# A new written-out order of the same work, and another choice of which engine scales which row

## The chip, the cores and the metric

The kernel runs on one core of a Trainium2 chip. The core has a matrix engine (PE, with its weight loads shown apart as PEld), a vector engine (DVE), an activation engine (ACT), GpSimd (POOL), a queue engine (SP), and sixteen DMA engines that move data between HBM and the on-chip memory. The metric is the device time of one execution in microseconds. Three executions of the kernel before took 898.75, 900.19 and 900.25 us, so its median is 900.19 us.

## The reference

The input `x` has 2048 tokens of width 576. Two results are made of it and mixed token by token with a gate:

```python
g = _sigmoid((x * gate_w).sum(-1, keepdims=True))
a = irfft2(rfft2(x) * (w_r + 1j * w_i))          # over tokens and width
q = einsum("nd,dhc->nhc", x, w_q)                # 32 heads, 2 x 128
s1, s2 = q1 @ k1.T, q2 @ k2.T                    # 64 scores each
e = argmax(s1) * 64 + argmax(s2)                 # one of 4096 experts
act = gelu(einsum("nd,nhd->nh", x, u[e]))
b = einsum("nh,nh,nhd->nd", softmax_of_one, act, v[e])
return g * a + (1 - g) * b
```

Part `a` is a two-dimensional Fourier filter. Part `b` picks, for each token and each of 32 heads, one row of `u` and one row of `v`, takes the dot product of the token with the `u` row, and sums the `v` rows weighted by the result. The softmax is over a single candidate.

## The kernel before

The 2048 tokens are 16 tiles of 128. The heads are cut into 8 chunks of 4. Each `u` row is stored next to its `v` row, so that one gather brings both: 128 rows of 1152 numbers, 4608 bytes each, into a slot called `uv`. There are 512 such gathers, one for each tile and head.

**Scores.** For each chunk `c`, `build_m` (L345 to L356) multiplies the query weights with the keys, and `scores` (L406) multiplies the token tiles with the result, two tiles at a time (`tp`). ACT and DVE find the index of the largest score (L415 to L453).

**Tiles 0 to 9** (`group`, L516 to L577). Four gathers are issued by POOL (L516), four dot products are taken on DVE (L523, "dots"), ACT applies gelu (L525), and the four `v` rows are weighted and summed. `ROWS[t][c]` says how. The value 16 means that PE sums them, with diagonal weights that ACT makes (L563). Otherwise bit k of the value means that row k is scaled on ACT (L548) and then added on DVE (L549); a bit that is not set means that DVE scales and adds in one instruction (L553). Tiles 0 and 1 (`T_T`) take another way in both kernels: ACT scales (L499), PE turns the rows and sums them in PSUM (`turned`), and DVE adds the result (L506).

**Tiles 10 to 15** (`quad`, L604 to L641). Here a gather holds four heads of 32 tokens. The indices are turned for that by sixteen small copies on ACT (`shuffle`, L462). The token tile is repeated (`repeat`, PE L594 and ACT L596). Then come the gathers (L604), the dots (L609), gelu (L610), the weights `a` (L611), a small diagonal `dg` (L613), and sixteen matmuls (L625) that add four rows to the sum of the tile. These last matmuls free the four `uv` slots.

**The filter.** `fold` (DVE L743 to L745, PE L752, ACT L754 and L755) prepares each of the 16 token tiles. When all are folded, `f2` (L764) begins the transform, followed by `f4`, `f5` and `f6` for each frequency group, and by `invert` (L904 and L914, with DVE L907 and L908) for each tile. `gates` (DVE L332) takes the dot product for the gate. `mix` (L930) joins both parts, `send` (L934) stores a tile, and `finish` (L639 to L641) does this in two halves for tile 15.

**The order.** All of this is first written down as 4337 jobs, numbered as they are created. The list `ORDER` holds the 4337 numbers. `follow` walks this list. Every engine carries out its own jobs strictly in the order of the list (each is tied to the one before it on its engine by a dependency without a semaphore); between engines only data and slots make one wait for another. The walk also hands out the slots: a job that needs a slot takes the one that has been free for longest in the list:

```python
for n, x in enumerate(seq):
    j = self.jobs[x]
    for b in j.bufs:
        if b.tag is None:
            b.tag = next(g for g in b.tags if self.rings.get(g))
            b.slot = self.rings[b.tag].popleft()
    for b in j.bufs:
        b.left -= 1
        if not b.left:
            self.rings[b.tag].append(b.slot)
```

So a change of the list changes which job of an engine comes first, and which earlier job a gather waits for before its slot is free. In the last third of the execution there are 18 `uv` slots: 12 of their own, two in areas that are free by then (one of them is shown in the profile as `area`), and four that held token tiles until their gates were taken (shown as `pair`).

The jobs that the prediction speaks of have these numbers in both lists: 3246 is the first matmul job of the filter's transform (`f2`, q = 0); 3495 to 3510 are the gate dots of tiles 0 to 15; 4283 is the PE job of tile 15, chunk 3; 4272 to 4275 are the four gathers of that chunk; 4276 to 4279 are their dots, 4281 is `a` and 4282 is `dg`; 4287 and 4291 are the gather and the dot of row 3 of chunk 4; 3627, 3662 and 3582 are the first PE jobs of `invert` for tiles 10, 15 and 5.

Of the kernel before, what the change touches and what calls it, by code (L numbers as in the profile page):

```python
# [969 lines left out]
ROWS = {0: (0, 16, 16, 15, 6, 2, 12, 0), 1: (0, 15, 0, 12, 5, 16, 5, 16), 2: (12, 8, 2, 6, 0, 8, 0, 1), 3: (2, 10, 0, 5, 0, 7, 4, 16), 4: (4, 0, 0, 6, 16, 7, 16, 0), 5: (2, 0, 1, 0, 0, 9, 12, 16), 6: (4, 15, 4, 8, 16, 0, 16, 14), 7: (8, 0, 16, 16, 6, 12, 9, 2), 8: (6, 16, 7, 0, 12, 16, 16, 11), 9: (4, 0, 0, 16, 0, 8, 16, 5)}  # L970
# [19 lines left out]
def is_d(t, c):  # L990
    return t < NE and ROWS[t][c] > 15


ORDER = [
# [214 lines left out]
```

## Time and profile before

| | us |
|---|---|
| median of three executions | 900.19 |
| the profiled execution, as timed | 900.38 |
| its span, from the first to the last instruction | 898.6 |
| PE busy | 856.3 |
| DVE busy | 811.5 |
| ACT busy | 596.3 |
| POOL busy | 570.3 |

The profiled execution lies 0.19 us above the median. Between its span and its time lie 1.8 us. Busy times are unions of the instructions' records; consecutive matmuls overlap in the records, so a PE that is shown as fully busy is fed without a gap, but a single matmul's duration is longer than the distance to the next one. A stretch in the table of windows shows, for each engine, its busy time and number of instructions, then the granted share of the PE clock, the mean busy share of the sixteen DMA engines and the rate in GB/s.

### The profile page before, as it was taken

How to read it: one execution, taken by the hardware profiler on the slowest of the kernel's cores; microseconds unless marked ns; L12 is line 12 of the kernel's file. 1: busy time of each engine (PE TensorE's matmuls, PEld its weight loads, DVE VectorE, ACT ScalarE, POOL GpSimd, SP SyncE). 2: the span in 40 equal slices, each digit the busy share in tenths (PEclk: the TensorE clock that was granted, in tenths of full speed). 3: DMA queues.
4: the chain of work that ended last, by engine and by line, in shares of the span. 5: the costliest groups of instructions: out<-in, count | busy, mean ns of one | idle time of the engine just before them, and what ended most of it. 6: DMA issues, size and time to landing. Idle time of an engine off the chain costs nothing. (4 is left out here: it accounts for less than half of the span.)

```text
span 898.6 us, 16947 instructions
## 1 busy us (share of the span) xinstructions
PE 856.3 (95%) x5502; PEld 661.0 (74%) x5502; DVE 811.5 (90%) x2022; ACT 596.3 (66%) x2067; POOL 570.3 (63%) x516
## 2 busy tenths in 40 slices
PE   6999999999999999999999999769889999899987
PEld 5888888888888778888888888657556676566554
DVE  3779999999999899999999999899999889877877
ACT  4999997877878688788879789773232434232322
POOL 0356556666677676676657776666767677777771
PEclk9999999999999999999999999859999999999999
DMA  9999999999999999999999999999999999999998
GB/s 299 349 332 367 379 345 367 349 372 361 380 357 368 377 386 384 376 388 357 394 359 368 415 350 397 418 370 365 402 415 420 419 402 419 420 420 419 418 419 340
DMA packets 89611, 342.44 MB, mean 381 GB/s; under 512 B 9969, under 2 KB 10865, under 8 KB 89522
## 3 DMA queue, kind: packets, MB, share of 16 engines
q0 software_dynamic: 73728, 302.02, 86.5%
q1 hardware_dynamic: 15794, 39.33, 11.9%
q8 instruction: 44, 0.72, 0.3%
q14 instruction: 45, 0.37, 0.1%
HBM read 336.59 MB, written 4.72 MB: 380 GB/s over the span
## 5 line engine op out<-in xcount | busy, mean ns | idle before, releaser
L516 POOL DMA_INDIRECT uv<-uv,ei x317 | 356.6, 1125 | 226.5 <-issue 46.6
L260 PE MATMUL bank<-mh,xt 128*128 128x512 f32 x768 | 269.8, 402 | 0.0
L422 ACT ACTIVATE area<-bank,area 128x64 bf16<-128x64 f32 x1008 | 220.3, 360 | 15.1 <-DVE area L415 10.9
L604 POOL DMA_INDIRECT uv<-uv,eiq x144 | 156.6, 1087 | 70.1 <-issue 23.3
L523 DVE SCALAR_TENSOR_TENSOR uv<-uv,pair 128x576 f32<-128x576 f32 x256 | 187.3, 750 | 12.5 <-DMA uv<-uv,ei 11.9
L260 PE MATMUL bank<-ml,xt 128*128 128x512 f32 x448 | 175.0, 391 | 0.0
L260 PEld LDWEIGHTS bank<-mh,xt 128*128 128x128 f32 x768 | 144.2, 188 | 30.3
L260 PE MATMUL bank<-mhx,xt 128*128 128x512 f32 x384 | 136.6, 399 | 0.1
L260 PE MATMUL bank<-uv,dg 128*32 128x288 f32 (+1 forms) x784 | 115.0, 412 | 4.3 <-DVE dg L613 4.2
L609 DVE SCALAR_TENSOR_TENSOR uv<-uv,xr 128x576 f32<-128x576 f32 x144 | 105.7, 751 | 12.4 <-DMA uv<-uv,eiq 12.1
L553 DVE SCALAR_TENSOR_TENSOR xn<-uv,a,xn 128x576 f32<-128x576 f32 x133 | 107.7, 811 | 0.2
L260 PE MATMUL bank<-fi,bt 128*128 128x289 f32 x384 | 101.7, 416 | 1.0 <-DVE area L908 1.0
L260 PEld LDWEIGHTS bank<-fi,bt 128*128 128x128 f32 x384 | 82.5, 243 | 20.6 <-issue 6.5
L260 PEld LDWEIGHTS bank<-ml,xt 128*128 128x128 f32 x448 | 84.3, 188 | 15.7
L260 PEld LDWEIGHTS bank<-uv,dg 128*32 128x32 f32 (+1 forms) x784 | 60.6, 131 | 35.7 <-DVE dg L613 10.1
L260 PEld LDWEIGHTS bank<-mhx,xt 128*128 128x128 f32 x384 | 72.1, 188 | 15.6 <-DVE area L371 0.5
L415 DVE TENSOR_REDUCE area<-bank 128x16 f32<-128x1024 f32 x63 | 76.6, 1217 | 4.3 <-PE bank L260 4.0
L260 PE MATMUL bank<-mlx,xt 128*128 128x512 f32 x192 | 75.0, 390 | 0.0
L430 ACT ACTIVATE area<-area 128x256 bf16<-128x256 bf16 x189 | 73.0, 437 | 1.1
L610 ACT ACTIVATE b<-z 128x4 f32<-128x4 f32 x48 | 9.9, 205 | 84.4 <-DVE uv L609 57.9
L260 PEld LDWEIGHTS bank<-kT,uv 128*64 128x64 f32 x1280 | 41.6, 141 | 18.2 <-issue 13.4
L260 PE MATMUL bank<-kT,uv 128*64 128x64 f32 x1280 | 46.5, 228 | 6.7 <-DMA uv<-wqT 6.7
(199 smaller groups left out, 1348.1 us busy)
## 6 DMA issues: line engine op xcount, KB each, us to landing
uv<-wqT SPq DMA_DIRECT2D x32, 512.0 KB, 6.5
uv<-uv,ei POOLq DMA_INDIRECT x317, 6.9
w<-wri SPq DMA_DIRECT2D x16, 289.0 KB, 6.7
pair<-xn SPq DMA_DIRECT2D x8, 288.0 KB, 6.2
uv<-uv,eiq POOLq DMA_INDIRECT x144, 8.6
out<-xn SPq DMA_DIRECT2D x8, 288.0 KB, 5.8
uv<-wq SPq DMA_DIRECT2D x8, 256.0 KB, 6.5
uv<-xT SPq DMA_DIRECT2D x8, 256.0 KB, 7.1
```

The lines of the kernel that those rows point to most:

```text
L260: after('PE', nc.tensor.matmul(*args, **kw))
L415: dv(dve(1024, True), lambda: nc.vector.tensor_reduce(mv.ap[:, 2 * tp:2 * tp + 2, :], ps.ap.rearrange('p a (g e) -> p a g e', e=E), AX.X, ...
L422: on('ACT', actv(sg.ap[:, j, g, :], ps.ap[:, j, g * E:g * E + E], AF.Sign, bias=mv.ap[:, 2 * tp + j, g:g + 1], scale=-1.0))
L430: ac(act(256), lambda b=b: actv(s2()[:, :, b * Q:b * Q + Q], s2()[:, :, b * Q:b * Q + Q], AF.Copy, bias=b / 4), [sg], [])
L516: on('POOL', nc.gpsimd.indirect_dma_start(out=g.ap.rearrange('p a d -> p (a d)'), out_offset=None, in_=uv, in_offset=bass.IndirectOffsetOn ...
L523: dv(0.68, lambda k=k, g=rows[k]: stt(g.ap[:, 0, :], g.ap[:, 0, :], 1.0, x.ap, op0=ALU.mult, op1=ALU.mult, accum_out=z.ap[:, k:k + 1]), [( ...
L553: dv(0.73, lambda v=v, s=s: stt(y.ap, v(), s(), y.ap, op0=ALU.mult, op1=ALU.add), [y], [(rows[k], 1), a])
L604: on('POOL', nc.gpsimd.indirect_dma_start(out=g.ap.rearrange('p a d -> p (a d)'), out_offset=None, in_=uv, in_offset=bass.IndirectOffsetOn ...
L609: dv(0.68, lambda j=j: stt(rows[j].ap[:, 0, :], rows[j].ap[:, 0, :], 1.0, xr[t][j].ap, op0=ALU.mult, op1=ALU.mult, accum_out=z.ap[:, j:j + ...
L610: ac(0.1, lambda: actv(b.ap, z.ap, AF.Gelu_apprx_tanh), [b], [(z, j) for j in range(HPC)], table='gelu')
```

## The change

Only two constants differ. In `ROWS`, 30 of the flags of tiles 2 to 9 are changed: 15 rows that ACT scaled are now scaled and added by DVE alone, and 15 go the other way. The number of flagged rows is 61 in both kernels, no entry of 16 appears or goes, and the entries of tiles 0 and 1 stay as they are. `ORDER` is another permutation of the same 4337 jobs; all 173 of its lines differ.

```diff
-ROWS = {0: (0, 16, 16, 15, 6, 2, 12, 0), 1: (0, 15, 0, 12, 5, 16, 5, 16), 2: (12, 8, 2, 6, 0, 8, 0, 1), 3: (2, 10, 0, 5, 0, 7, 4, 16), 4: (4, 0, 0, 6, 16, 7, 16, 0), 5: (2, 0, 1, 0, 0, 9, 12, 16), 6: (4, 15, 4, 8, 16, 0, 16, 14), 7: (8, 0, 16, 16, 6, 12, 9, 2), 8: (6, 16, 7, 0, 12, 16, 16, 11), 9: (4, 0, 0, 16, 0, 8, 16, 5)}
+ROWS = {0: (0, 16, 16, 15, 6, 2, 12, 0), 1: (0, 15, 0, 12, 5, 16, 5, 16), 2: (12, 2, 2, 6, 4, 2, 0, 1), 3: (2, 10, 0, 0, 0, 7, 6, 16), 4: (2, 0, 0, 6, 16, 7, 16, 8), 5: (2, 0, 3, 8, 6, 9, 12, 16), 6: (4, 5, 0, 9, 16, 0, 16, 12), 7: (8, 0, 16, 16, 6, 9, 9, 2), 8: (0, 16, 6, 8, 12, 16, 16, 10), 9: (4, 0, 8, 16, 0, 4, 16, 5)}
...
 ORDER = [
-    21, 22, 0, 1, 23, 2, 3, 77, 4, 78, 9, 16, 6, 10, 89, 90, 80, 7, 5, 79, 133, 20, 91, 11, 13, 81, 83, 84, 128, 92, 97, 82, 86, 87, 8, 98, 85, 17,
...
+    3608, 3588, 4295, 3596, 3587, 4303, 4314, 3581, 4304, 4305, 3666, 4306, 4316, 3563, 3543, 3890, 4317, 4307, 3597, 4318, 4326, 3598, 3633, 3599,
+    4328, 4329, 4330, 4222, 4223, 3778, 4319, 3589, 3668, 3779, 3590, 3667, 4331, 4334, 4332, 4335, 4333, 4336,
 ]
```

What stands where in the two lists can be counted from them. Counted per engine, the median job of PE and of POOL moves by 2 places among the jobs of its engine, the median job of DVE and of ACT by 3. Jobs of each engine listed ahead of some jobs (before / after):

| ahead of | PE | DVE | ACT | POOL |
|---|---|---|---|---|
| the last job of the scores (tile 14) | 820 / 820 | 923 / 925 | 871 / 873 | 298 / 300 |
| 3246, the first job of `f2` | 853 / 854 | 1038 / 1040 | 971 / 974 | 328 / 331 |
| the first sum of tile 12 | 909 / 908 | 1217 / 1209 | 1063 / 1059 | 397 / 397 |
| the first sum of tile 14 | 961 / 962 | 1363 / 1364 | 1139 / 1142 | 462 / 461 |
| 4283, the sum of tile 15, chunk 3 | 1001 / 1000 | 1464 / 1461 | 1193 / 1192 | 506 / 510 |

343 rows, old and new, of the table ORDER are left out of this document.

## Prediction

> **What bounds the kernel now.** I read the page's first line and the list of waits, then the table of windows, and then the timelines at the two places where the table shows that something breaks.
>
> ```profile
> span 898.6 us, 16947 instructions
> PE bank L260 <- DMA uv<-wqT: 6.7, 1, 6.7
> ...
> 270.00:360.00 90.00, 89.78 (x567) 73.30 (x566) 85.03 (x203) 71.90 (x267) 59.75 (x53) 1.00 0.99 379
> ...
> 450.00:540.00 90.00, 90.00 (x519) 73.71 (x515) 87.67 (x216) 73.69 (x286) 60.76 (x56) 1.00 0.99 373
> ```
>
> PE waits 6.7 us for its first weights and is then fed almost without a gap until 540 us; the poorer of these two windows lacks 0.22 us in 90, and it is the poorest. An order can't do better there with the same matmuls, only worse. What is left to win lies behind 540 us, in 358 us.
>
> ```profile
> 540.00:560.00 20.00, 19.23 (x120) 16.69 (x118) 19.31 (x51) 18.16 (x65) 12.51 (x12) 1.00 1.01 395
> 560.00:580.00 20.00, 15.34 (x92) 12.68 (x92) 16.46 (x49) 17.41 (x72) 13.02 (x13) 0.99 1.03 416
> 580.00:600.00 20.00, 12.34 (x52) 10.24 (x52) 20.00 (x52) 12.74 (x40) 11.07 (x11) 0.59 0.98 370
> 600.00:611.00 11.00, 9.89 (x47) 6.58 (x45) 10.30 (x29) 7.75 (x23) 6.44 (x6) 0.53 1.00 379
> 611.00:630.00 19.00, 18.15 (x110) 14.60 (x106) 17.99 (x54) 7.51 (x30) 14.44 (x14) 1.00 0.97 372
> 630.00:675.00 45.00, 39.15 (x232) 26.17 (x233) 44.04 (x114) 14.00 (x36) 31.49 (x30) 1.00 1.02 409
> 675.00:720.00 45.00, 44.72 (x271) 30.91 (x270) 40.38 (x103) 15.84 (x37) 32.46 (x30) 1.00 1.03 420
> 720.00:855.00 135.00, 130.64 (x811) 85.00 (x810) 110.62 (x308) 45.42 (x117) 101.89 (x93) 1.00 1.02 416
> 855.00:877.00 22.00, 17.69 (x103) 11.08 (x102) 16.13 (x46) 5.00 (x14) 15.40 (x16) 1.00 1.03 418
> 877.00:898.60 21.60, 16.13 (x119) 8.71 (x117) 17.00 (x46) 6.06 (x17) 3.19 (x3) 0.96 0.85 337
> ```
>
> Three stages are to be seen. From 560 to 611 us the scores are over, PE idles for 13.4 us (51 less 15.34, 12.34 and 9.89), its clock is granted at about half, and DVE is full from 580 on: DVE is late with the folds, and `f2` can't begin before the last of them. From 630 to 877 us the DMA engines are busy all the time and move 409 to 420 GB/s, where the two windows of the scores above have 379 and 373; gathers are the bound there. Behind 877 us the last rows are summed.
>
> **The change part by part.** `ROWS` moves 30 flags and leaves their number at 61. A row scaled by DVE alone costs 811 ns, one scaled on ACT costs DVE 750 ns:
>
> ```profile
> L553 DVE SCALAR_TENSOR_TENSOR xn<-uv,a,xn 128x576 f32<-128x576 f32 x133 | 107.7, 811 | 0.2
> L549 DVE TENSOR_TENSOR xn<-uv,xn 128x576 f32<-128x576 f32 x60 | 44.9, 750 | 1.3 <-ACT uv L548 1.2
> ```
>
> Fifteen rows go each way, 15 x 0.06 = 0.9 us of DVE out and in, so this sums to nothing; what hides it besides is PE, the bound of the stage where nearly all these rows lie. If that cover is gone it costs or brings up to 0.9 us.
>
> *Up to 560 us* I put 0. The first three loads on SP (the fifth weight block, the keys, the first weight block) are the same in both lists, so PE starts at 6.7 us again; and at the last score job both lists have 820 PE jobs behind them, with 923 and 925 on DVE. Below there is only the 0.22 us quoted. Above: DVE has 2.3 to 5 us of slack in each 90 us window; an order that let PE wait for 1% of that stage would cost 5 us. I take 0, being nearest to the rows.
>
> *The folds, 560 to 611 us.* DVE sets the end, so I count its jobs ahead of job 3246: 1038 before, 1040 after. By line, two gate dots (L332) and one dot (L609) more, and one tiny L449 less. Consecutive dots start 0.68 us apart (first two rows); the other rows are DVE's waits for gathers between 540 and 611 us (total, times, longest) and the start of `f2`:
>
> ```profile
> 608.28 0.75 DVE L332 SCALAR_TENSOR_TENSOR pair<-pair,t 128x576 f32<-128x576 f32 x1
> ...
> 608.96 0.75 DVE L332 SCALAR_TENSOR_TENSOR pair<-pair,t 128x576 f32<-128x576 f32 x1
> DVE uv L523 <- DMA uv<-uv,ei: 2.7, 3, 1.1
> 610.94 6.23 PE L260 MATMUL bank<-fi,bt 128*128 128x289 f32 x24
> ```
>
> That is 3 x 0.68 - 0.1 = 1.9 us, and `f2` begins at 612.9 instead of 610.94. The 2.7 us of waits are three dots whose gather had not landed when their turn came, with folds queued behind them on DVE; in the new list such dots may wait less or more. From -2.7 to +2.7 us I take 0 for that, as the list doesn't tell when a gather lands.
>
> *Gathers.* Ahead of job 3246 the old list has 328 gathers, the new one 331. The trace agrees with the list for before: up to 611 us POOL had issued 316 + 13 (the groups of that stretch, below) and one each into a `pair` and the `area` slot, 331. Three more are behind us when the gather-bound stage begins. Each brings 302.02 / 512 = 0.59 MB, at the 420 GB/s of the window from 675 us 1.40 us:
>
> ```profile
> q0 software_dynamic: 73728, 302.02, 86.5%
> L516 POOL DMA_INDIRECT uv<-uv,ei x316 | 355.4, 1125 | 226.2 <-issue 46.6 <-PE bank L260 35.9 <-DVE xn L553 31.4
> L604 POOL DMA_INDIRECT uv<-uv,eiq x13 | 13.8, 1059 | 12.1 <-ACT uv L548 3.5 <-DVE uv L523 1.9 <-DVE a L611 1.8
> ```
>
> So 3 x 1.40 = 4.2 us less is left, and it starts 1.9 us later: **-2.3 us**. If the extra three merely wait in the queue behind the same slots, it is 0 instead of -4.2.
>
> *The end.* The last two gathers need slots that job 4283 (the sum of tile 15, chunk 3) frees, in both lists. Rows of three engines' timelines:
>
> ```profile
> 859.46 1.06 POOL L604 DMA_INDIRECT pair<-uv,eiq  x1 [0.30 <-DMA uv<-uv,eiq]
> 870.50 0.76 DVE L609 SCALAR_TENSOR_TENSOR pair<-pair,xr 128x576 f32<-128x576 f32 x1 [3.03 <-DMA pair<-uv,eiq]
> 875.84 0.28 DVE L613 TENSOR_TENSOR dg<-rp,a 128x128 f32<-128x128 f32 x1
> 876.55 3.09 PE L260 MATMUL bank<-fi,bt 128*128 128x289 f32 x12
> 879.57 0.43 PE L260 MATMUL bank<-uv,dg 128*32 128x288 f32 x1
> 880.68 2.25 PE L260 MATMUL bank<-t,krb 128*128 128x289 f32 x8
> 881.00 1.05 POOL L604 DMA_INDIRECT uv<-uv,eiq  x1 [3.28 <-PE bank L260]
> ```
>
> The last gather of chunk 3 is the 15th from the end. It goes out at 859.46 and lands at 870.50, 11.0 us later. `dg` is ready at 876.1 (875.84 + 0.28), but the PE list has an `invert` (job 3627, 3.09 us) ahead of job 4283, whose 1.1 us end at 880.68; POOL had stood still for 3.28 us. In the new list the last gather of chunk 3 (4275) is the 12th from the end. Its `dg` is listed behind the dot 4291, whose gather 4287 goes out three places later: 3 x 1.40 = 4.2 us, then the dot's 0.68, `dg` 0.28 and the sum's 1.1, together 6.3 us from landing. With 11.0 us to land, the slots are free 17.3 us after the issue of 4275; the stream itself reaches the last two gathers after 10 x 1.40 = 14.0 us. The wait would be 3.3 us, as before. With the 8.6 us that is the median for such gathers it would be 0.9:
>
> ```profile
> uv<-uv,eiq POOLq DMA_INDIRECT x144, 8.6
> ```
>
> I take **-1.0 us**, between 0 and -2.4, nearer to 0 because the queue is fullest there.
>
> **The sum:** 0 + 1.9 - 4.2 - 1.0 = -3.3 us. The profiled execution would come to 900.38 - 3.3 = 897.1; the median, 0.19 lower, to 896.9 us.
>
> **The rivals.**
>
> *The lists are the same list.* The gain is two small differences of counts, at one point each. At the first sum of tile 12 both have 397 gathers ahead, at that of tile 14 they have 462 and 461: the lead of three is gone there by the list. If the stream is the bound this can't be (a gather that has been made isn't made again); if slots are the bound, the lead is worth nothing. For slots speaks that POOL, too, waits for PE in the late stage:
>
> ```profile
> POOL uv L604 <- PE bank L260: 22.6, 28, 3.3
> ```
>
> Against it speaks the flat 416 to 420 GB/s. Then the time is 900.2 us, within about 1.5.
>
> *Two transforms ahead of the last sum: slower.* In the new PE list two `invert` jobs (3662 and 3582, 3.09 us each) stand right before 4283, where the old one has only 3627. If they begin when the previous sum ends, they fill PE's time while chunk 3 lands. If the first has to wait for a free PSUM bank, chunk 3's `dg` is ready and its sum stands behind them. Before, issue to end of sum took 880.7 - 859.5 = 21.2 us. The issue is now three places later, 3 x 1.40 = 4.2 us; with the same 21.2 us the last gathers move by 4.2 - 2.3 = +1.9 us, and the time is 900.19 + 1.9 = 902.1 us, slower. It decides from 21.2 - 4.2 + 2.3 = 19.3 us on; I reckon 17.3. With all of the second transform exposed, 3.09 more, it is 905 us.
>
> *The clock isn't lowered.* The half clock follows PE's long idle time:
>
> ```profile
> 566.85 2.50 PE L260 MATMUL bank<-kr,f 128*128 128x128 f32 x20
> ...
> 581.95 4.61 PE L260 MATMUL bank<-kr,f 128*128 128x128 f32 x20 [4.52 <-ACT eiq L462]
> ...
> 604.86 4.63 PE L260 MATMUL bank<-kr,f 128*128 128x128 f32 x20 [1.05 <-ACT xr L596]
> ```
>
> The last two folds ahead of `f2` take 4.63 us at half clock and would take 2.50 at full, so `f2` would begin 2.1 us earlier, and the time is 896.9 - 2.1 = 894.8 us. The new list puts two `repeat` jobs of PE into the stretch that was idle for 4.52 us. But between the next two folds (tiles 11 and 10) it has no PE job at all and about 6 us of DVE work, so I expect the clock to fall there. The Trainium skill, "TensorE: Matmul & The Clock Gate", section "What's actually happening", says that the clock falls to half after about 3.4 us of idleness and rises after as much activity; by that rule the 6 us lower it again, and only an order that splits every gap below 3.4 us gives the 894.8.
>
> **How the numbers follow.** Chances: the forecast 0.38; the same list 0.27; the end slower 0.20; the clock kept 0.10; PE waiting somewhere in the score stage 0.05, slower by 5 us. A measurement of this kernel tells about 0.2% from no change, 1.8 us. Faster by more than that are the forecast and the kept clock, less what of the first falls short of 1.8 us, with a little from the edge of the second: 0.48. Within 0.2% lie most of the second and that short part, 0.27. Slower are the last two kinds, 0.25. The predicted time is that of the likeliest, 896.9 us. The range: down to 890.5, which is the kept clock with the waits of the folds gone as well (894.8 - 2.7) and the end at its best (-1.4 more): 890.7; up to 905, the second transform exposed, or PE starved by 1% of its stage. Its own range for the forecast is 894.5 to 899.
>
> **What would show it.** PE's windows up to 540 us full again, within 0.5 us each, or the first step is wrong. The first `f2` matmul at 611 to 615 us, with 333 to 335 gathers issued by then; fewer, and the lead was none. 180 gathers from there at 416 to 420 GB/s; if the rate falls, slots and not the stream were the bound. At the end, a wait of POOL of 1 to 3.3 us ahead of the second to last gather; if the sum of chunk 3 stands behind two transforms with its `dg` long ready, the slower rival holds. The half clock again between 580 and 611 us. Wrong altogether it would be if PE showed idle time in the score stage, or if time moved at a place that I have not counted, such as the sums of tiles 11 to 14.

## The result, and the profile after

| | before | after |
|---|---|---|
| median, us (four executions each) | 900.22 | 895.17 |
| lowest to highest, us | 898.75 to 901.16 | 893.84 to 895.93 |
| the profiled execution as timed, us | 900.38 | 894.79 |
| its span, us | 898.6 | 892.9 |

The ratio is 0.9944, with a 95% interval of 0.9925 to 0.9962: 5.0 us faster, where 3.3 us were forecast, and 895.17 us where the forecast was 896.9. The profiled executions differ by 5.6 us, their spans by 5.7.

First the table of windows of the changed kernel, in the stretches of before (the columns are as there; the last stretch ends with the span):

```profile
270.00:360.00 90.00, 90.00 (x571) 74.44 (x570) 86.32 (x208) 73.17 (x272) 59.98 (x54) 1.00 0.99 374
...
450.00:540.00 90.00, 90.00 (x529) 73.62 (x528) 87.27 (x217) 75.83 (x284) 60.88 (x56) 1.00 1.00 384
540.00:560.00 20.00, 19.96 (x122) 17.43 (x120) 19.58 (x51) 18.77 (x77) 11.88 (x12) 1.00 1.02 404
560.00:580.00 20.00, 14.13 (x90) 11.79 (x88) 18.47 (x55) 14.31 (x58) 16.05 (x13) 1.00 1.03 417
580.00:600.00 20.00, 15.19 (x57) 10.75 (x57) 20.00 (x52) 16.76 (x52) 12.99 (x13) 0.60 0.99 391
600.00:611.00 11.00, 9.16 (x46) 7.23 (x47) 10.96 (x34) 5.11 (x18) 7.35 (x7) 0.65 0.97 348
611.00:630.00 19.00, 17.42 (x104) 13.80 (x104) 17.66 (x53) 6.78 (x28) 14.47 (x14) 1.00 1.01 401
630.00:675.00 45.00, 43.08 (x250) 28.98 (x253) 44.13 (x112) 14.11 (x36) 33.58 (x31) 1.00 1.03 418
675.00:720.00 45.00, 44.16 (x278) 28.89 (x278) 39.30 (x104) 19.31 (x44) 33.03 (x31) 1.00 1.02 419
720.00:855.00 135.00, 129.31 (x809) 84.32 (x808) 111.71 (x306) 43.59 (x115) 95.33 (x93) 1.00 1.03 419
855.00:877.00 22.00, 19.46 (x112) 12.71 (x111) 16.79 (x50) 3.92 (x12) 13.90 (x14) 1.00 1.02 416
877.00:892.90 15.90, 9.98 (x85) 5.28 (x84) 11.95 (x32) 5.27 (x14) 0.00 (x0) 0.94 0.82 303
```

PE is full up to 540 us, as before. The first difference that counts is in DVE's column between 560 and 580 us: 18.47 us busy instead of 16.46. From 540 to 611 us DVE is busy for 69.0 us (19.58 + 18.47 + 20.00 + 10.96) where it was 66.1, so 2.9 us of its idle time are gone, in the stretch of the folds. What follows stands in POOL's column: 13 gathers instead of 11 between 580 and 600 us, 7 instead of 6 between 600 and 611. POOL's timeline says why (start, duration, and in brackets the idle time and its cause). Its longest waits between 560 and 611 us before:

```profile
570.59 1.27 POOL L516 DMA_INDIRECT uv<-uv,ei  x1 [1.93 <-PE bank L260]
...
583.97 0.93 POOL L604 DMA_INDIRECT uv<-uv,eiq  x1 [1.90 <-DVE uv L523]
588.38 1.25 POOL L604 DMA_INDIRECT uv<-uv,eiq  x1 [3.47 <-ACT uv L548]
```

and after:

```profile
583.68 1.38 POOL L604 DMA_INDIRECT uv<-uv,eiq  x1 [2.28 <-ACT uv L548]
...
589.10 1.14 POOL L604 DMA_INDIRECT uv<-uv,eiq  x1 [1.34 <-DVE xn L553]
```

Waits of over 1 us come six times in that stretch before, 12.25 us in all, and four times after, 6.05 us in all; each ended with a job of PE, DVE or ACT. Then the rate: 401 and 418 GB/s where 372 and 409 had been.

How many gathers are out is read from POOL's groups of instructions up to 611 us (line, engine, operation, tiles, count, busy us, mean ns, idle time before):

```profile
L516 POOL DMA_INDIRECT uv<-uv,ei x316 | 354.0, 1120 | 225.7 <-issue 43.6 <-PE bank L260 34.1 <-ACT area L379 31.4
L604 POOL DMA_INDIRECT uv<-uv,eiq x16 | 18.1, 1132 | 10.1 <-ACT uv L548 2.3 <-issue 2.1 <-DVE xn L553 1.7
L604 POOL DMA_INDIRECT area<-uv,eiq x2 | 2.1, 1072 | 0.6 <-issue 0.6
```

316 + 16 + 2 = 334, three more than the 331 of before. DVE's waits from 540 to 611 us have one row for gathers that had not landed (total, times, longest), 1.4 us instead of 2.7:

```profile
DVE uv L523 <- DMA uv<-uv,ei: 1.4, 2, 0.8
```

PE's timeline shows the last two folds (`kr,f`), the beginning of a sum between them (`uv,dg`), and the first `f2`:

```profile
599.84 2.50 PE L260 MATMUL bank<-kr,f 128*128 128x128 f32 x10
603.54 0.70 PE L260 MATMUL bank<-uv,dg 128*32 128x288 f32 x2 [1.20 <-ACT bt L754]
...
605.62 2.40 PE L260 MATMUL bank<-kr,f 128*128 128x128 f32 x10
607.86 0.38 PE L260 MATMUL bank<-ident,tw 128*128 128x128 f32 x2
608.88 4.52 PE L260 MATMUL bank<-fi,bt 128*128 128x289 f32 x17 [0.64 <-ACT bt L754]
```

`f2` begins at 608.88 us, 2.1 us earlier than before. It waits for ACT's copy of the last fold. Behind PE's last long wait stand a sum and one fold; in the old list it was two folds and a sum.

At the end, POOL's timeline:

```profile
857.40 1.42 POOL L604 DMA_INDIRECT pair<-uv,eiq  x1 [0.30 <-DMA uv<-uv,eiq]
...
866.87 0.97 POOL L604 DMA_INDIRECT uv<-uv,eiq  x1 [1.69 <-PE bank L260]
...
874.37 0.93 POOL L604 DMA_INDIRECT uv<-uv,eiq  x1 [2.52 <-PE bank L260]
875.61 0.94 POOL L604 DMA_INDIRECT uv<-uv,eiq  x1 [0.30 <-issue]
```

The last issue is at 875.61 us, 6.75 earlier than before. 13 gathers start behind 855 us where 17 did. So the lead is three gathers at 611 us and four at 855 us, or 4.2 and 5.6 us at the 1.40 us of a gather; the span ends 5.7 us earlier. By these two traces, all of the gain is there before the end begins. Another trace of the old order divides it otherwise: the kernel of experiment 3 below (the store experiment) has the old list up to 854 us, and it had issued 332 gathers at 611 us and started 15 behind 855. Against it the lead is two gathers at both places, and its span of 897.7 us is 4.8 us longer than that of the changed kernel.

One thing is new that the prediction doesn't speak of, the output stores. The store queue's timeline before (start, us to the end of the group, tiles, count):

```profile
834.57 12.25 SPq L934 DMA_DIRECT2D out<-xn  x2
854.44 0.33 SPq L934 DMA_DIRECT2D out<-xl  x1
854.82 0.43 SPq L934 DMA_DIRECT2D out<-xn  x1
855.29 0.44 SPq L934 DMA_DIRECT2D out<-xw  x1
856.15 28.67 SPq L934 DMA_DIRECT2D out<-xn  x2
```

and after:

```profile
824.89 8.34 SPq L934 DMA_DIRECT2D out<-xn  x2
853.91 23.08 SPq L934 DMA_DIRECT2D out<-xl  x2
877.36 3.31 SPq L934 DMA_DIRECT2D out<-xn  x4
880.77 0.53 SPq L934 DMA_DIRECT2D out<-xw  x1
881.35 0.76 SPq L934 DMA_DIRECT2D out<-xl  x1
```

A group of two shows that the second store waited: before, four stores went out at 854.4 to 856.2 us, among gathers that were queued for the engines. In the new list the store of tile 12 stands ahead of them. Its `mix` (job 4000) ends at 876.6 us, and six stores whose rows were ready before stand behind it on the same queue until all gathers are issued. To see what that does, the gathers were timed by their packets: each has 73728 / 512 = 144, so gather N is in when 144 N packets of the software queue have ended.

```
gather in, us          330th    480th    500th    512th   end of span
before                 613.2    839.2    871.3    890.5   898.6
after                  608.7    833.4    863.2    884.1   892.9
after minus before      -4.6     -5.8     -8.1     -6.4    -5.7
```

From the 480th to the 500th the new kernel gains 2.3 us, and gives 2.4 back by the end of the span. The same count shows where the lead begins. The 305th gather came in at 571.6 us before and at 570.8 after, 0.8 us earlier; the 320th at 596.7 and at 592.2, 4.5 us earlier. Against the kernel of experiment 3 (570.6 and 596.1) it is -0.2 and 3.9 us. So most of the lead arises between 571 and 592 us, whichever trace of the old order is taken.

### The profile page after: what moved, and what is told of

Same layout as the page of the kernel before. It is cut to its first block, busy times and chain, and to the rows that moved or that the text cites. A ratio compares the mean times of both kernels' runs of the same rounds, so it can differ in the third digit from the quotient of the medians.

```text
span 892.9 us, 16949 instructions
## 1 busy us (share of the span) xinstructions
PE 855.1 (96%) x5502; PEld 661.0 (74%) x5502; DVE 808.7 (91%) x2022; ACT 597.2 (67%) x2067; POOL 564.7 (63%) x516
## 3 DMA queue, kind: packets, MB, share of 16 engines
q0 software_dynamic: 73728, 302.02, 86.7%
## 4 chain that ended last, share of the span: by engine, by line
PE 76%; DVE 12%; DMA 8%; issue 2%; ACT 2%; POOL 0%; DVEq 0%; SPq 0%; ACTq 0%; POOLq 0%
PE bank L260 76%; DMA uv<-uv,eiq 5%; DVE uv L609 4%; DMA uv<-uv,ei 1%; DMA pair<-uv,eiq 1%; DVE pair L609 1%; DVE t L810 1%; DVE xn L553 1%; DVE uv L523 1%; DMA uv<-wqT 1%; DVE area L609 1%; DVE dg L613 1%; DVE t L809 0%; DVE xn L549 0%; ACT bt L866 0%
## 5 line engine op out<-in xcount | busy, mean ns | idle before, releaser
L604 POOL DMA_INDIRECT uv<-uv,eiq x142 | 152.1, 1071 | 63.7 <-issue 21.9
L553 DVE SCALAR_TENSOR_TENSOR xn<-uv,a,xn 128x576 f32<-128x576 f32 x135 | 109.2, 810 | 0.3 <-ACT xn L551 0.3
L415 DVE TENSOR_REDUCE area<-bank 128x16 f32<-128x1024 f32 x63 | 76.7, 1217 | 5.7 <-PE bank L260 5.3
L430 ACT ACTIVATE area<-area 128x256 bf16<-128x256 bf16 x189 | 70.9, 425 | 1.1
```

Of the source, the lines that this page charges most:

```text
L415: dv(dve(1024, True), lambda: nc.vector.tensor_reduce(mv.ap[:, 2 * tp:2 * tp + 2, :], ps.ap.rearrange('p a (g e) -> p a g e', e=E), AX.X, ...
L430: ac(act(256), lambda b=b: actv(s2()[:, :, b * Q:b * Q + Q], s2()[:, :, b * Q:b * Q + Q], AF.Copy, bias=b / 4), [sg], [])
L553: dv(0.73, lambda v=v, s=s: stt(y.ap, v(), s(), y.ap, op0=ALU.mult, op1=ALU.add), [y], [(rows[k], 1), a])
L604: on('POOL', nc.gpsimd.indirect_dma_start(out=g.ap.rearrange('p a d -> p (a d)'), out_offset=None, in_=uv, in_offset=bass.IndirectOffsetOn ...
```

## The experiments

The experiments ran on four chips. On three of them the old kernel itself took 932 to 937 us, and the intervals there reach about half a per cent to either side; only the store experiment was on a chip where the old kernel took 900. The changed kernel itself was not run on these four chips.

**1. Where the lists part.** Two kernels join the lists behind the first job of `f2`, 3246. The first has the new `ROWS` and begins with the new list; the other has the old `ROWS` and begins with the old one. Jobs of rows that differ are renumbered to match.

```diff
+head = NEW[:NEW.index(3246) + 1]
+ORDER = head + [x for x in OLD if x not in head]
```

> The new list up to and with the first matmul job of f2, then what is left in the order of the old list, with the new ROWS. Theory 1, the stream: the gathers run about 4.6 us ahead of the old kernel's when f2 begins (the 330th had come in at 613.2 us in the old kernel's trace, at 608.7 in the changed one's), and as the stream is the bound from there, the lead is kept: 900.2 - 4.6 = 895.6 us, 894.5 to 897, the 500th gather 4 to 5 us ahead of before. Rival, the slots: behind f2 the list is again the old one, slots are freed by the old list's jobs, so the lead melts: 900.2 us within 1.5, the 500th gather within 1.5 us of before.

> The old list up to and with the first matmul job of f2, then what is left in the order of the new list, with the old ROWS. Theory 1, the stream: only what the two traces show behind f2 is won, 5.7 - 4.6 = 1.1 us: 899.1 us, 898 to 900.5; f2 begins at 611 us as before. Rival: the late order carries the gain (slots freed earlier behind f2), then 895 to 896.5 us.

> The kernel of new_to_f2 once more, since the kernel before took 932 us on the chip of that call and its gathers came in at less than 400 GB/s behind f2; on a chip on which before takes 900 us the theories can be told apart. The stream: 895.6 us, 894.5 to 897 (0.995 of before), and the 330th and the 500th gather each 4 to 5 us ahead of before. The slots: 900.2 us within 1.5, the 500th gather within 1.5 us of before.

> The kernel of old_to_f2 once more, for the same reason. The stream: 899.1 us, 898 to 900.5 (0.999 of before). Rival: the late order carries the gain, 895 to 896.5 us (0.995); on the chip of the first call it came out at 0.993, which speaks for the rival.

> The new list up to and with the first matmul job of f2, then the old order, for the third time: on the chips of the first two calls before took 932 and 936 us and the intervals were half a per cent wide; on a chip on which before takes 900 us they are 0.1. The stream: the lead of the gathers at f2 (4.6 us at the 330th) is kept to the end, 895.6 us, 894.5 to 897 (0.995 of before). The slots: the lead melts behind f2, 900.2 us within 1.5 (1.000), as the pooled 0.9993 of the first two calls suggests.

> The old list up to f2, then the new order, for the third time, for the same reason. The stream: 899.1 us, 898 to 900.5 (0.999 of before). Rival, the late order carries the gain: 895 to 896.5 us (0.995), as the pooled 0.9946 of the first two calls suggests; then the 330th gather comes in as late as before, at 613 us, and the lead must grow between the 330th and the 512th gather, to 4 us or more.

| ratio to before, 95% interval | first (before 932.2) | second (936.4) | third (936.6) | pooled |
|---|---|---|---|---|
| new list up to `f2` | 0.9995 (0.9952 to 1.0038) | 0.9991 (0.9934 to 1.0047) | 0.9963 (0.9916 to 1.0011) | 0.9983 (0.9955 to 1.0011) |
| new list from `f2` on | 0.9927 (0.9884 to 0.9969) | 0.9974 (0.9924 to 1.0024) | 0.9981 (0.9937 to 1.0026) | 0.9959 (0.9933 to 0.9985) |

The pooled ratios weigh each by the inverse square of its interval's half width. Together they make 0.17 + 0.41 = 0.58%, near the whole change in the result (0.56%), but each is uncertain by almost 0.3%. They fall the other way round than the first theory has it: it asked for 0.9949 and 0.9988. Both lie just outside the pooled intervals; the rival's 1.000 and 0.995 lie inside. This speaks against the first theory on these chips, but it doesn't test it, since its premise isn't seen there. With the old list, `f2` began at 620.7, 620.6 and 620.1 us in the three traces, with the new one at 621.1, 619.5 and 622.1: no earlier. In the 50 us ahead of `f2`, POOL's waits of over 1 us sum up to 7.0, 10.8 and 11.9 us with the old list and to 10.8, 9.5 and 10.7 us with the new one. The halving that the chip of the result shows (12.25 to 6.05 us) isn't there. Nor is there a steady stream behind `f2`, as windows of the third run of the new list up to `f2` show:

```profile
700.00:720.00 20.00, 17.12 (x102) 11.11 (x104) 12.39 (x32) 5.80 (x15) 11.19 (x12) 0.91 0.96 374
720.00:740.00 20.00, 18.61 (x110) 13.37 (x103) 17.41 (x45) 6.79 (x20) 12.30 (x12) 1.00 0.98 373
...
800.00:820.00 20.00, 16.70 (x103) 10.32 (x105) 11.95 (x32) 6.95 (x18) 9.15 (x9) 0.83 0.77 277
```

The gathers move 277 to 374 GB/s here, with the engines 77 to 98% busy, and POOL issues 9 to 12 in 20 us where the stream of the profile before takes 14. That is not the steady stream on which the theory rests.

**2. Rows or order.** One kernel has the new `ROWS` with the old order, one the old `ROWS` with the new order. A scaling job that the other list doesn't hold was put up to 12 places ahead of its addition.

```diff
-ROWS = {... 2: (12, 8, 2, 6, 0, 8, 0, 1), 3: (2, 10, 0, 5, 0, 7, 4, 16), ...}
+ROWS = {... 2: (12, 2, 2, 6, 4, 2, 0, 1), 3: (2, 10, 0, 0, 0, 7, 6, 16), ...}
```

> The new ROWS with the old order; where a row is now scaled on ACT, that job stands up to 12 places ahead of its addition on DVE. If the rows are worth nothing, as 15 go each way: 900.2 us within 1.5. If the choice of rows carries the gain (DVE finds less to wait for between 540 and 611 us): 895 to 897 us. If ACT delivers late at the changed rows, which were placed without regard to ACT's queue: up to 15 waits of some 0.3 us in the scores, 900 to 903 us.

> The new order with the old ROWS, the scaling jobs on ACT placed in the same way. If the order carries the whole: 895.2 us within 1.5, the 330th gather at 608 to 610 us. If the rows carry it: 899 to 901 us.

> The kernel of order_only once more, on a chip on which before takes 900 us. If the order carries the whole: 895.2 us within 1.5 (0.9944). If the rows carry it: 899 to 901 us. On the chip of the first call it came out at 0.9975.

The rows alone came out at 1.0106 (1.0067 to 1.0145), slower. The order alone came out at 0.9975 (0.9935 to 1.0015) and 0.9983 (0.9933 to 1.0032), pooled 0.9978 (0.9947 to 1.0009), which holds no gain at all and has 0.9944 just outside. The rows are not what makes the kernel faster by themselves: put into a list that wasn't made for them, with their scaling jobs where I put them, they cost 1%. DVE's waits for ACT's scaling (the third expectation for the rows) are not the cause; in that run's list of waits they have one row of any size:

```profile
DVE xn L549 <- ACT uv L548: 0.5, 1, 0.5
```

Its trace doesn't show the loss where the changed rows stand: `f2` begins at 618.2 us, earlier than in the three traces of the old list with the old rows above. Its gathers fall behind later, between the 350th (in at 652.6 us) and the 400th (742.2 us, against 733.2 to 739.0 in those three). What costs it the 1% isn't settled.

**3. The stores.** The old kernel with only the store queue's order changed, on a chip where before took 900.41 us:

```diff
-SP: ... 3626, 3890, 3572, 3543, 3581, 3563, 4112, 4223, 3590, 3617, 4001, ...
+SP: ... 3626, 4001, 3890, 3572, 3543, 3581, 3563, 4112, 4223, 3590, 3617, ...
```

> The old kernel, with only the order on the store queue changed: the store of tile 12, whose rows are finished at 877 us, goes ahead of the stores of tiles 11, 3, 0 and 4, so that these four, which went out at 854.4 to 856.2 us, are held behind it until the last gathers are under way, as in the new order. Theory: four stores of 0.295 MB are 1.18 MB, 2.8 us at 420 GB/s, and the gathers 480 to 500 come in that much sooner, 29.3 to 29.8 us for twenty instead of 32.1; the last two gathers share the engines with the held stores and lose up to 1.5 us of it again; the time falls by 1.3 to 2.8 us, to 0.997 to 0.9985 of before. Rival: stores are a side stream that costs the gathers nothing, twenty gathers take 32.1 us as before, and the time is 1.000; or the held stores end the span, and it is slower.

The ratio is 1.0002 (0.9992 to 1.0013): no difference. The store queue's timeline shows that the hold worked, as the stores begin at 873 us instead of 854:

```profile
873.03 1.69 SPq L934 DMA_DIRECT2D out<-xl  x2
874.75 0.50 SPq L934 DMA_DIRECT2D out<-xn  x1
875.68 0.33 SPq L934 DMA_DIRECT2D out<-xw  x1
```

The gathers timed by their packets:

```
gather in, us       330th    480th    500th    512th   480-500   500-512
before              613.2    839.2    871.3    890.5     32.1      19.2
stores held         612.5    836.8    865.9    889.6     29.1      23.7
```

The twenty gathers take 29.1 us instead of 32.1, as the theory said. But the last twelve take 4.5 us more, not up to 1.5, and nothing is left. So the first half of the theory fits (a store takes its bytes from the gathers) and its conclusion is wrong. From the 330th gather to the last the engines moved 414 and 416 GB/s in the two kernels, which fits that a store costs its bytes wherever it stands ahead of that. The Trainium skill, "DMA: Bandwidth & Descriptors", section "Issuing engines are not separate DMA queues", says that the queues of all issuers run on the same sixteen engines; the 29.1 and 23.7 us agree.

This run has a second use. Up to its held stores its list is the old one, and yet its `f2` begins 1.3 us earlier (609.65 instead of 610.94) and its 480th gather comes 2.4 us earlier than in the trace of before. By so much do two traces of one order differ in the middle. Of the 1.3 us, 0.6 are the last two folds on PE, which took 4.04 us instead of 4.63, as the granted clock rose earlier there (0.81 instead of 0.53 from 600 to 611 us).

**4. The end.** The changed kernel with the end put in another order:

```diff
-3662, 3582, 4320, 4298, 4291, 3583, 4282, 3657, 4283, 3658, 4315,
+3662, 4320, 4298, 3657, 4282, 3658, 4291, 4283, 3582, 3583, 4315,
```

> The changed kernel, with the end put in another order: dg of tile 15, chunk 3 goes ahead of the dot of row 3 of chunk 4, behind which it had waited, the sum of chunk 3 goes ahead of the second transform (tile 5), and DVE's first addition for tile 14 ahead of both. In the changed kernel's trace POOL stood still for 2.52 us ahead of the second last gather, and the last two gathers came in 3.8 us later than the stream's pace. Theory: the wait goes, the last gather comes in 2 to 3 us earlier, and DVE uses 1.4 us in which it waited for the dot's gather; the time falls by 1 to 1.5 us, to 0.993 of before. Rival: DVE is full from 872 us on and its work is the same, so nothing is won: 0.9944. Slower by up to 1 us if the second transform is now late for DVE.

> The kernel of end_dg again, on a chip on which before takes 900 us. Theory: no wait of POOL over 1 us ahead of the last two gathers, the time 1 to 1.5 us under that of the changed kernel, 893.7 to 894.2 us (0.993 of before). Rival: the held stores and the last gathers share the engines (in the run on held stores the last twelve gathers took 23.7 us instead of 19.2) and DVE is full from 872 us on, so an earlier issue of the last two gathers wins nothing: 895.2 us within 0.7 (0.9944).

It came out at 0.9946 (0.9896 to 0.9995) and 0.9947 (0.9884 to 1.0010) of before, pooled 0.9946 (0.9907 to 0.9985); this holds the theory's 0.993 and the rival's 0.9944. POOL's wait did go, as its timeline in the second run shows for the last two gathers:

```profile
915.03 0.94 POOL L604 DMA_INDIRECT uv<-uv,eiq  x1 [0.30 <-issue]
916.37 0.94 POOL L604 DMA_INDIRECT uv<-uv,eiq  x1 [0.40 <-issue]
```

0.40 us stand where the changed kernel has 2.52. But this execution took 941.76 us, with gathers that came in later throughout, and there is no trace of the changed kernel from that chip. So it isn't shown that the new order of the end took the wait away, nor that anything is gained by it. No version that beats the changed kernel was found.

## Why the prediction was right, and where not

**Faster, by a lead of gathers: right.** Three gathers more were forecast ahead of `f2`, 333 to 335 by then; 333 were out when it began and 334 at 611 us. Behind it the rate is 401 to 419 GB/s, and the lead doesn't melt, which speaks for the stream. The slots aren't ruled out: from 611 us on the gathers of tiles 10 to 15 wait for PE for 26.6 us in all, where it was 25.1 before.

**The score stage at 0: right.** PE's windows are full in both, and its first wait is 6.8 us instead of 6.7.

**The folds at +1.9 us: wrong, and this is the step that failed.** `f2` begins 2.1 us earlier than in the trace of before (0.8 us earlier than in that of the store experiment), not 1.9 later, and outside the 611 to 615 us that were named as a sign. I had counted DVE's jobs in the list ahead of `f2` and charged their time to it. But `f2` doesn't wait for those jobs. In the new list six gate dots (L332) stand ahead of it; when it began at 608.88 us, two of them had been taken and the third had just started (608.83). `f2` waits for what stands ahead of it on PE and for ACT's copy of the last fold (the 0.64 us `<-ACT bt L754` in its row). Before, the two folds that begin at 604.86 us stood directly ahead of it, and then a sum that begins with this row and ends at 611.02:

```profile
609.42 0.70 PE L260 MATMUL bank<-uv,dg 128*32 128x288 f32 x3
```

In the new list the fold before the last is over at 602.34 us, the sum at 605.70, and only one fold is left. The last subtraction of the folds on DVE comes 1.1 us earlier, too (before it began at 605.52 us):

```profile
604.42 0.42 DVE L745 TENSOR_TENSOR f<-xl 128x255 f32<-128x255 f32 x1
```

But PE waits for it in neither trace. Before, it ended at 605.94 us, five us ahead of `f2`, while PE was still in the two folds; after, it ended at 604.84, while PE was in the sum. So the reading that DVE's last fold sets the end was wrong already for the trace of before. DVE may still bear on it earlier: what ended PE's wait ahead of the two folds is ACT's copy (L596) by the trace of before, and DVE's row addition (L553) by that of the store experiment.

The 0 that I took for DVE's waits, between -2.7 and +2.7, was off as well: DVE lost 2.9 us less, and the trace of the store experiment, with 66.0 us busy from 540 to 611 us, agrees with before on this. With the gathers at -4.2 the two steps were to make -2.3 us. At 611 us on the clock the new kernel is three gathers ahead, which is -4.2, and by the packets -4.6 (two gathers and -3.8 against the store experiment). The lead appears where POOL stands still less (6.05 us in waits of over 1 us instead of 12.25; 12.66 in the store experiment). That DVE's fewer idle microseconds are what lets POOL go on sooner is read from the windows and was not shown by a run; experiment 1 was to show it and could not.

**Nothing between 611 and 855 us: a little short, or right.** By the trace of before a fourth gather is won there, 1.4 us, with the rate at 401 and 418 GB/s in the windows where it had been 372 and 409. But the store experiment, with the old order, has 379 and 418 in these windows, and against it no gather is won there. So the fourth gather is within what two traces of one order differ by.

**The end at -1.0 us: the wait right, the worth open.** The wait of POOL was forecast at 0.9 to 3.3 us and is 2.52. The mechanism can be followed in the rows of DVE and PE:

```profile
871.91 0.76 DVE L609 SCALAR_TENSOR_TENSOR uv<-uv,xr 128x576 f32<-128x576 f32 x1 [1.36 <-DMA uv<-uv,eiq]
...
872.60 0.28 DVE L613 TENSOR_TENSOR dg<-rp,a 128x128 f32<-128x128 f32 x1
```

```profile
866.55 6.12 PE L260 MATMUL bank<-fi,bt 128*128 128x289 f32 x24
872.94 0.44 PE L260 MATMUL bank<-uv,dg 128*32 128x288 f32 x3 [0.27 <-DVE dg L613]
```

`dg` stands behind the dot of 4291, which waited 1.36 us for its gather, and the two transforms fill PE's time until just before, 866.55 to 872.67 us. From the issue of 4275 (857.40) to the end of the sum, 874.1, it is 16.7 us, where 17.3 were reckoned and 19.3 would have made it slower. So the rival of the two transforms fell, but narrowly: they ended about 0.2 us before `dg` did (872.88 us). By the trace of before, the wait saved and spent comes to 0.1 us and not 1.0: 5.6 us were won up to 855 us, and 5.7 at the end. Against the store experiment the new kernel is 3.4 us ahead at the 480th gather and 4.8 us at the end of the span, so the worth of the end isn't settled. A second wait of 1.69 us stands four places earlier, and the held stores run beside the last gathers.

**The clock that isn't lowered: fell.** The windows from 580 to 611 us have 0.60 and 0.65, where before had 0.59 and 0.53. It is lowered again, a little shorter. The stretch of about 6 us without a PE job, from which this was expected, isn't in the trace: PE's longest idle time between 562 and 611 us is 3.75 us, up to 579.14.

**The sum.** Forecast 0 + 1.9 - 4.2 - 1.0 = -3.3 us; measured, by the profiled executions, about 0 - 4.2 up to 611 us, -1.4 up to 855 and -0.1 at the end, -5.7 in the span. That the median came within 1.7 us of the forecast is in part luck: the +1.9 didn't come, the -1.4 wasn't counted, and the end brought 0.9 less than its -1.0. What was right is the way the time moved and, by the trace of before, the gathers' term, the largest of the sum.

What stays open: which part of the new list shortens POOL's waits between 560 and 611 us, how the 5 us divide between the list ahead of `f2` and behind it on a chip where the old kernel takes 900 us, and what the new `ROWS` are worth in the new order.

## What to carry to other kernels

Count what an engine does in a stretch, not what stands ahead of a job in a list: a job waits for its own inputs and for its own engine, and the place of another engine's work in the list is no time. In the store experiment, with the transfer engines full to the last gather, holding stores back moved the wait and not the end; by this reading only work that lets the stream start earlier, or keeps it from a gap, is worth something there. Before a gain of a few microseconds is divided among stages, take two traces of the same order: here they differ by 1.3 and 2.4 us in the middle. Measure an order that is worth half a per cent on a chip where the old kernel runs as in its profile; on the others the intervals were too wide for it.

## What the runs showed of the hardware

On three chips the old kernel took 932 to 937 us instead of 900. In the third run of the new list up to `f2`, on one of them, the gathers are slower, 277 to 374 GB/s in the windows shown above, against 419 to 420 in two of these stretches of the store experiment:

```profile
700.00:720.00 20.00, 19.83 (x121) 13.87 (x120) 18.08 (x46) 7.85 (x22) 14.14 (x13) 1.00 1.03 419
...
800.00:820.00 20.00, 20.00 (x124) 13.11 (x126) 14.43 (x43) 3.92 (x12) 15.43 (x16) 1.00 1.02 420
```

The difference isn't only behind `f2`: from 20 to 540 us PE is busy for 515.5 us in that run, where it is 519.7 in the trace of before and 520.0 in that of the changed kernel.

The Trainium skill, "HBM Reference", section "Specifications (TRN2)", says that two cores share a memory domain, that a core streaming alone reaches about 425 GB/s and that each gets about 358 when both stream. The 420 agree with the first. That another core was active on the three slower chips would fit, but no trace here shows one.
